# Fourier mixing and a hardswish MLP on one core: the first pair of batches reordered, weights converted in pairs and two phases, forward rows on SP's queue, scratch writes by Scalar

## The chip, the core and the metric

The kernel runs on one core of a Trainium2 chip. The metric is the device time of one execution in microseconds (us), the median of several runs, lower is better. TensorE does the matmuls (PE in the profile, PEld its weight loads), DVE is VectorE, ACT is ScalarE, POOL is GpSimd, SP the engine that mostly issues transfers. The granted clock is the share of TensorE's full clock that the profile records for a stretch; 0.50 is called half clock below. The DMA share is the mean busy share of the core's 16 DMA engines, so the share times 16 is a number of engines; it can come out slightly above 1.

## The reference

A two-dimensional Fourier transform over sequence and features, of which the real part goes through a two-layer MLP:

```python
X = np.fft.fft(x, axis=1)              # x: (8, 3008, 256) float32
X = np.fft.fft(X, axis=2)
h = X.real.reshape(24064, 256) @ w_in  # w_in: (256, 2048)
g = h * np.clip(h + 3.0, 0.0, 6.0) / 6.0
out = g @ w_out                        # w_out: (2048, 256)
```

The weights arrive as float64. The kernel computes in float32, so it takes their bits apart with integer operations and puts float32 together ("narrowing").

## The kernel before

The sequence length is split as 47 x 64. Batches are worked in four pairs. For a pair, **stage 1** transforms over 47 in eight pieces; each piece needs four forward rows of x and four mirrored ones for 94 row groups (2 batches x 47). The mirrored ones come by an indirect transfer, the "gather". The result z goes to a scratch in DRAM (`zd`), is read back transposed (`g`), and **stage 2** finishes the transform. The feature transform is folded into w_in beforehand. The MLP then runs in steps: `mlp1` (first layer and gating), `combine` on POOL, `mlp2` (second layer, by a seven-product scheme whose mixed weights are `G`). Later pairs' stage 1 runs beside the MLP of the pair before; only the first pair stands alone, and the conversion of all weights falls into that time.

```python
def load_x(pr, c):                       # two x buffers, both transfers on POOL's queue
    xt = xpool.tile([PR, 2 * XC, D], F32, tag="x", name="xt")      # PR = 94
    nc.gpsimd.dma_start(out=xt[:, 0:n, :], in_=rows[:, c * XC + 1:c * XC + 1 + n, :])
    ...
    nc.gpsimd.indirect_dma_start(out=xt[:, XC:, :]..., in_=x_r,
        in_offset=bass.IndirectOffsetOnAxis(ap=IX[:, i:i + 1], axis=0))

def narrow(st, o):                       # one tile of weights, eight operations, all on DVE
    ts(top[:], hi, 0xFFFFF, 0x100000, op0=AL.bitwise_and, op1=AL.bitwise_or)
    ts(low[:], lo, 8, 0xFFFFFF, op0=AL.logical_shift_right, op1=AL.bitwise_and)
    stt(frac[:], low[:], 2.0 ** -24, top[:], op0=AL.mult, op1=AL.add)
    ts(ex[:], hi, 20, 0x7FF, op0=AL.logical_shift_right, op1=AL.bitwise_and)
    ts(ex[:], ex[:], 1023.0 - 127.0, 0.0, op0=AL.subtract, op1=AL.max)
    ts(ex[:], ex[:], 255.0, 2.0 ** 23, op0=AL.min, op1=AL.mult)
    stt(ex[:], hi, -2 ** 31, ex[:], op0=AL.bitwise_and, op1=AL.bitwise_or)
    stt(o, frac[:], 2.0 ** -20, ex[:].bitcast(F32), op0=AL.mult, op1=AL.mult)

for c in range(NXC):                     # stage 1 of the first pair; NXC = 8
    for part, eng in enumerate((nc.gpsimd, nc.vector)):
        fold(first, c, part, eng)        # add forward and mirrored rows: POOL, then DVE (y)
    if c + 2 < NXC:
        load_x(first, c + 2)
    for i in range(XC // 2):
        stage1(first, c, i)              # TensorE, copy of z by ACT, scratch write by SP
    narrow_w_in(c)
    ...
```

After stage 1 come the first two w_out tiles, stage 2, and the main loop; the other six w_out tiles are narrowed one per step in steps 0 to 5. In the timelines shown here POOL, DVE and Scalar each work through their own instructions in program order.

Of the kernel before, what the change touches and what calls it, by code (L numbers as in the profile page):

```python
# [40 lines left out]

N1, N2 = 47, 64
# [6 lines left out]
def kernel(  # L49
# [10 lines left out]
    nc = tc.nc  # L60
# [19 lines left out]
    xpool = ctx.enter_context(tc.tile_pool(name="xpool", bufs=2))  # L80
# [21 lines left out]
    T = consts.tile([P, 2, NK1, 2, N2], F32, name="T")  # L102
# [14 lines left out]



    def load_x(pr, c):  # L120
        xt = xpool.tile([PR, 2 * XC, D], F32, tag="x", name="xt")
        rows = x_pn[pr.p * PR:(pr.p + 1) * PR]
        n = XC if c < NXC - 1 else XC - 1
        nc.gpsimd.dma_start(out=xt[:, 0:n, :], in_=rows[:, c * XC + 1:c * XC + 1 + n, :])
        if n < XC:
            nc.gpsimd.dma_start(out=xt[:, n:XC, :], in_=rows[:, 0:1, :])
        i = pr.p * NXC + c
        nc.gpsimd.indirect_dma_start(
            out=xt[:, XC:, :].rearrange("p n d -> p (n d)"), out_offset=None, in_=x_r,
            in_offset=bass.IndirectOffsetOnAxis(ap=IX[:, i:i + 1], axis=0),  # L130
        )
        pr.x[c] = xt

    def fold(pr, c, part, eng):
        xt = pr.x[c]
        n = XC if c < NXC - 1 else XC - 1
        a, r = xt[:, 0:n, :], xt[:, 2 * XC - 1:2 * XC - 1 - n:-1, :]
# [7 lines left out]
        lo, hi = xt[:, 0:XC, 1:P], xt[:, 0:XC, D - 1:P:-1]  # L145
# [3 lines left out]
        if n < XC:  # L149
            h = xt[:, XC, :]  # L150
            tt(y[:, XC, 1:P], h[:, 1:P], h[:, D - 1:P:-1], op=AL.add)
            tt(y[:, XC, P + 1:D], h[:, 1:P], h[:, D - 1:P:-1], op=AL.subtract)
            eng.tensor_copy(y[:, XC, 0:P + 1:P], h[:, 0:P + 1:P])
            eng.tensor_copy(y[:, n, 0:P + 1:P], xt[:, n, 0:P + 1:P])
# [10 lines left out]
    def stage1(pr, c, i):  # L165
# [18 lines left out]
        if i == XC // 2 - 1:  # L184
            nc.sync.dma_start(
                out=pr.zd[:].rearrange("b k c n d -> (b k c) n d")[:, c * XC:(c + 1) * XC, :],
                in_=z[:],
            )
            del pr.y[c], pr.z[c]
# [11 lines left out]
    def stage2(pr, gr, i):  # L201
# [5 lines left out]
        for u in range(2):  # L207
            kk = 2 * i + u
            for blk in range(2):
                nc.tensor.matmul(ps[:, blk, 2 * u:2 * u + 2], g[:, kk, blk * P:(blk + 1) * P],  # L210
                                 T[:, blk, gr * 2 * KK + kk], start=True, stop=True)
        nc.scalar.copy(pr.q[gr][:, :, 4 * i:4 * i + 4, :], ps[:])

    def stage2n_mul(pr, gr):

        shape = [P, 2 * KK, 2 * N2]
        m = spool.tile(shape, F32, tag="m", name="m")
        t0 = T[:, 0, gr * 2 * KK:(gr + 1) * 2 * KK].rearrange("p k b n -> p k (b n)")
        nc.gpsimd.tensor_tensor(m[:], t0, pr.g[gr][:, :, P:P + 1].to_broadcast(shape), op=AL.mult)
        pr.pr[gr] = m  # L220

    def stage2n_sum(pr, gr):
        m = pr.pr.pop(gr)
        ps = bank([P, 2 * TB], "ps3")
        nc.tensor.matmul(ps[:], ones[:], m[:].rearrange("p k n -> p (k n)"), start=True, stop=True)  # L225
# [74 lines left out]
    def mlp2(ch, fc):  # L300
# [3 lines left out]
        for i, mv in enumerate(moving):  # L304
# [5 lines left out]
            if fc == NF - 1 and (i % 2 == 1 or i == 6):  # L310
# [3 lines left out]
                nc.scalar.copy(ch.e[:, k:i + 1, 0:ch.n], ch.acc[i // 2][:, 0:i + 1 - k, 0:ch.n])  # L314
# [37 lines left out]
    nc.sync.dma_start(out=F[:], in_=c_stage1)  # L352
    nc.vector.tensor_copy(IX[:], F[0:PR, 5 * PZ:])
    for c in range(2):
        load_x(first, c)
    nc.sync.dma_start(out=C[:], in_=c_dim.rearrange("(h p) d -> p h d", p=P))
# [3 lines left out]
    wide = moe_w_in.dtype != F32  # L360
    WB = 512

    def load_w(src, dst):
        if not wide:
            nc.sync.dma_start(out=dst, in_=src)
            return None
        st = wpool.tile([P, 2 * WB], I32, tag="st", bufs=3, name="st")
        o = st[:].bitcast(moe_w_in.dtype)
        if len(src.shape) == 3:
            o = o.rearrange("p (c j) -> p c j", c=src.shape[1])  # L370
        nc.sync.dma_start(out=o, in_=src)
        return st

    def narrow(st, o):


        if st is None:
            return
        words = st[:].rearrange("p (n two) -> p n two", two=2)
        lo, hi = words[:, :, 0], words[:, :, 1]  # L380
        ts, stt = nc.vector.tensor_scalar, nc.vector.scalar_tensor_tensor
        top = wpool.tile([P, WB], I32, tag="top", name="top")
        low = wpool.tile([P, WB], I32, tag="low", name="low")
        ex = wpool.tile([P, WB], I32, tag="ex", name="ex")
        frac = wpool.tile([P, WB], F32, tag="frac", name="frac")
        ts(top[:], hi, 0xFFFFF, 0x100000, op0=AL.bitwise_and, op1=AL.bitwise_or)
        ts(low[:], lo, 8, 0xFFFFFF, op0=AL.logical_shift_right, op1=AL.bitwise_and)  # L387
        stt(frac[:], low[:], 2.0 ** -24, top[:], op0=AL.mult, op1=AL.add)  # L388
        ts(ex[:], hi, 20, 0x7FF, op0=AL.logical_shift_right, op1=AL.bitwise_and)
        ts(ex[:], ex[:], 1023.0 - 127.0, 0.0, op0=AL.subtract, op1=AL.max)  # L390
        ts(ex[:], ex[:], 255.0, 2.0 ** 23, op0=AL.min, op1=AL.mult)
        stt(ex[:], hi, -2 ** 31, ex[:], op0=AL.bitwise_and, op1=AL.bitwise_or)  # L392
        stt(o, frac[:], 2.0 ** -20, ex[:].bitcast(F32), op0=AL.mult, op1=AL.mult)

    w_in = {}

    def load_w_in(j):
        n, i = j // 2, j % 2
        w = wpool.tile([P, WB], F32, tag="w", bufs=5, name="w_in")
        w_in[n, i] = w, load_w(moe_w_in[i * P:(i + 1) * P, n * WB:(n + 1) * WB], w[:])  # L400

    def narrow_w_in(j):
        w, st = w_in[j // 2, j % 2]
        narrow(st, w[:])


    w_out = {}

    def load_w_out(j):
        w = wpool.tile([P, WB], F32, tag="w", bufs=5, name="w_out")  # L410
        rows = moe_w_out[2 * j * P:2 * (j + 1) * P, :].rearrange("(c p) d -> p c d", p=P)
        w_out[j] = w, load_w(rows, w[:].rearrange("p (c d) -> p c d", c=2))

    def narrow_w_out(j):
        w, st = w_out[j]
        narrow(st, w[:])

    def mix_w_out(j):
        bs = [w_out[j + i * (NWO // 2)][0][:].rearrange("p (c q h e) -> h p c q e", c=2, h=2, e=DH) for i in range(2)]
        b11, b12, b21, b22 = bs[0][0], bs[0][1], bs[1][0], bs[1][1]  # L420
        w = [G[:, i, 2 * j:2 * j + 2, :].rearrange("p c (q e) -> p c q e", e=DH) for i in range(7)]
        t2 = wpool.tile([P, 2, DB, DH], F32, tag="t2", name="t2")
        tt = nc.vector.tensor_tensor
        nc.scalar.copy(w[0], b11)
        nc.scalar.copy(w[1], b21)
        nc.scalar.copy(w[6], b22)
        tt(w[3], b11, b12, op=AL.subtract)
        tt(t2[:], b22, w[3], op=AL.add)
        tt(w[2], t2[:], b21, op=AL.subtract)
        tt(w[4], b22, b12, op=AL.subtract)  # L430
        nc.scalar.mul(w[5], t2[:], -1.0)

    NWI, NWO = 2 * FF // WB, NFC // 2
    for j in range(2):
        load_w_in(j)
    for b in range(2):
        nc.vector.memset(T[(1 - b) * N2:(2 - b) * N2, :, :, b], 0.0)
        nc.scalar.dma_start(out=T[b * N2:(b + 1) * N2, :, :, b], in_=c_stage2)
    nc.vector.memset(half[:], 0.5)
    nc.gpsimd.memset(ones[:], 1.0)  # L440

    def fold_w_in(n):

        cs = slice(n * 512, (n + 1) * 512)
        for blk in range(2):
            ps = bank([P, 512], "wps")
            for i in range(2):
                nc.tensor.matmul(ps[:], C[:, i, blk * P:(blk + 1) * P], w_in[n, i][0][:],
                                 start=(i == 0), stop=(i == 1))
            nc.scalar.copy(W1[:, blk, cs], ps[:])  # L450
        ps = bank([P, 512], "wns")
        for j in range(512 // P):
            for i in range(2):
                nc.tensor.matmul(ps[:, j:j + 1], w_in[n, i][0][:, j * P:(j + 1) * P], C[:, i, D:D + 1],
                                 start=(i == 0), stop=(i == 1))
        nc.scalar.copy(WN[:, n * (512 // P):(n + 1) * (512 // P)], ps[:, 0:512 // P])

    for c in range(NXC):
        for part, eng in enumerate((nc.gpsimd, nc.vector)):
            fold(first, c, part, eng)  # L460
        if c + 2 < NXC:
            load_x(first, c + 2)
        for i in range(XC // 2):
            stage1(first, c, i)
        narrow_w_in(c)
        if c + 2 < NWI:
            load_w_in(c + 2)
        if c % 2:
            fold_w_in(c // 2)
    ORDER = [0, NWO // 2, 1, NWO // 2 + 1, 2, NWO // 2 + 2, 3, NWO // 2 + 3]  # L470
    for j in ORDER[0:2]:
        load_w_out(j)
    load_g(first, 0)
    load_g(first, 1)
    for i in range(2):
# [3 lines left out]
    for j in range(2):  # L479
        narrow_w_out(ORDER[j])  # L480
        load_w_out(ORDER[j + 2])
    mix_w_out(0)
# [6 lines left out]
    def beside(p):  # L489
# [6 lines left out]
        if p == 0:  # L496
            for j in range(2, NWO):
                put(j - 2, narrow_w_out, ORDER[j])
                if j + 2 < NWO:
                    put(j - 2, load_w_out, ORDER[j + 2])  # L500
                if j % 2:
                    put(j - 2, mix_w_out, j // 2)
# [61 lines left out]
def _tables(B, S, D):  # L564
# [14 lines left out]
    for b in range(2):  # L579
# [21 lines left out]
        "c_stage2": t.reshape(N2, 2, NK1, N2).astype(np.float32),  # L601
        "c_dim": d.astype(np.float32),
# [32 lines left out]
```

## Time and profile before

| | before |
|---|---|
| time, median of 3 runs first given | 2096.5 us (2095.32 to 2096.98) |
| TensorE busy | 1985.9 us, 95% of the span |
| TensorE busy, first 200 us | 110.9 us |
| last fold result y of stage 1 | 98.4 us |
| first gating on DVE | 120.1 us |
| second layer of step 6 (seventh `acc` group) starts | 198.7 us |

From about 200 us on TensorE is full (199.32 us busy of the 200 from 400 to 600 us, at a granted clock of 1.00) and the rest of the work is fixed, so the three last rows serve as mile marks throughout. I call the stretch to the first mark part A, between the first and second part M, between the second and third part B. (The first mark is the start of the last but one DVE operation of the last y, always the same one; the prediction counts from an operation some 0.3 us earlier, 98.1.) Lines of this profile stand in the prediction.

### The profile page before, as it was taken

The page shows a single profiled execution, that of the slowest core. Times are in us where ns is not written, and L with a number is a line of the kernel's source. Part 1 is how long each engine was busy: PE and PEld are TensorE (multiplying, and loading weights), DVE is VectorE, ACT ScalarE, POOL GpSimd, SP SyncE. Part 2 cuts the span into 40 slices and gives each one's busy share as a digit, 9 for nine tenths or more (in the row PEclk, how much of TensorE's full clock was granted, in tenths as well). Part 3 has the DMA queues.
Part 4 walks back from the last instruction along what each step waited for, and adds up shares of the span by engine and source line. Part 5 has one row for each costly group of instructions (what it writes and reads, how often), then busy time and mean ns, then how long its engine had stood idle before and what let it go on. Part 6 is the DMA issues. An engine that isn't in the chain of part 4 may idle for free.

```text
span 2095.7 us, 28082 instructions
## 1 busy us (share of the span) xinstructions
PE 1985.9 (95%) x9136; PEld 1698.7 (81%) x9136; DVE 1495.8 (71%) x2768; ACT 671.6 (32%) x1157; POOL 1474.1 (70%) x1637
## 2 busy tenths in 40 slices
PE   3666999999999999999999999999999999999997
PEld 1355888888888888888888888888888888888886
DVE  4588676777677677667677667777677777777775
ACT  1122333333333333333333333333333333333332
POOL 3333887788667788778767787787866766766765
PEclk9678999999999999999999999999999999999999
DMA  6430121112101112112101111111020010010000
GB/s 160 133 110 10 43 54 48 50 37 49 28 21 34 43 33 61 47 38 52 35 21 30 42 38 43 42 51 47 23 48 11 14 26 21 16 26 21 16 16 19
DMA packets 163377, 86.81 MB, mean 41 GB/s; under 512 B 138496, under 2 KB 151040, under 8 KB 163232
## 3 DMA queue, kind: packets, MB, share of 16 engines
q1 hardware_dynamic: 128896, 58.71, 11.4%
q0 software_dynamic: 28160, 24.73, 4.4%
q10 hardware_dynamic: 6176, 1.57, 0.4%
q8 instruction: 74, 1.21, 0.3%
q14 instruction: 71, 0.58, 0.1%
HBM read 47.65 MB, written 37.22 MB: 40 GB/s over the span
## 4 chain that ended last, share of the span: by engine, by line
PE 88%; DVE 5%; DMA 4%; ACT 1%; POOL 1%; issue 1%; SPq 0%; DVEq 0%; POOLq 0%; ACTq 0%
PE acc L308 52%; PE v L254 15%; PE u L254 15%; DMA xt<-in_x_dram,IX 3%; PE ps L210 2%; PE ps L182 2%; DVE a L286 1%; PE ps L225 1%; ACT t L283 1%; DVE u L267 1%; DVE s L259 0%; DVE frac L388 0%; DVE low L387 0%; DMA g<-zd 0%; DVE ex L392 0%
## 5 line engine op out<-in xcount | busy, mean ns | idle before, releaser
L298 POOL TENSOR_TENSOR c<-a 128x512 f32<-128x512 f32 (+1 forms) x384 | 479.2, 1248 | 447.2 <-DVE a L286 257.2
L308 PE MATMUL acc<-c,G 128*128 128x256 f32 (+1 forms) x3072 | 714.0, 375 | 0.0
L308 PEld LDWEIGHTS acc<-c,G 128*128 128x128 f32 x3072 | 579.7, 191 | 73.9
L283 ACT ACTIVATE t<-u,half 128x512 f32<-128x512 f32 (+2 forms) x416 | 272.2, 654 | 1102.5 <-DVE u L267 1090.8
L259 DVE SCALAR_TENSOR_TENSOR s<-qn,WN,u 128x256 f32<-128x256 f32 x768 | 334.7, 477 | 365.1 <-PE u L254 364.5
L308 PE MATMUL acc<-a,G 128*128 128x256 f32 (+1 forms) x2304 | 557.5, 379 | 0.0
L308 PEld LDWEIGHTS acc<-a,G 128*128 128x128 f32 x2304 | 439.8, 192 | 58.7
L254 PE MATMUL v<-q,W 128*128 128x256 f32 x1536 | 402.3, 385 | 31.7 <-DVE a L286 31.7
L254 PE MATMUL u<-q,W 128*128 128x256 f32 x1536 | 395.0, 379 | 0.0
L254 PEld LDWEIGHTS v<-q,W 128*128 128x128 f32 x1536 | 292.6, 192 | 80.3 <-issue 35.3
L254 PEld LDWEIGHTS u<-q,W 128*128 128x128 f32 x1536 | 287.9, 190 | 65.8 <-issue 20.7
L286 DVE SCALAR_TENSOR_TENSOR a<-t,u 128x512 f32<-128x512 f32 (+2 forms) x416 | 266.2, 646 | 99.2 <-ACT t L283 94.0
L298 POOL TENSOR_TENSOR c<-a,c 128x256 f32<-128x256 f32 (+1 forms) x384 | 276.2, 719 | 30.1
L298 POOL TENSOR_TENSOR c<-c,a 128x256 f32<-128x256 f32 (+1 forms) x384 | 274.9, 716 | 30.1
L267 DVE TENSOR_TENSOR u<-s,v 128x512 f32<-128x512 f32 (+1 forms) x384 | 263.0, 685 | 41.1 <-PE v L254 1.3
L283 ACT ACTIVATE t<-v,half 128x512 f32<-128x512 f32 (+1 forms) x384 | 256.9, 669 | 5.5 <-DVE v L273 4.5
L273 DVE TENSOR_TENSOR v<-v,s 128x512 f32<-128x512 f32 (+1 forms) x384 | 257.7, 671 | 1.1
L286 DVE SCALAR_TENSOR_TENSOR a<-t,v 128x512 f32<-128x512 f32 (+1 forms) x416 | 255.1, 620 | 0.4 <-ACT t L283 0.2
L182 PE MATMUL ps<-y,F 94*96 94x512 f32 x120 | 73.7, 712 | 59.9 <-DVE y L148 53.8
L298 POOL TENSOR_TENSOR r<-w,e 128x256 f32<-128x256 f32 (+1 forms) x96 | 92.2, 981 | 3.8
L314 ACT COPY e<-acc 128x512 f32<-128x512 f32 (+1 forms) x192 | 86.3, 540 | 2.9 <-PE acc L308 2.8
L182 PEld LDWEIGHTS ps<-y,F 94*96 94x96 f32 x120 | 20.7, 186 | 80.3 <-issue 34.3
(68 smaller groups left out, 856.3 us busy)
## 6 DMA issues: line engine op xcount, KB each, us to landing
out_dram<-o SPq DMA_DIRECT2D x736, 32.0 KB, 1.6
zd<-z SPq DMA_DIRECT2D x32, 384.0 KB, 3.0
g<-zd SPq DMA_DIRECT2D x48, 256.0 KB, 3.9
xt<-in_x_dram POOLq DMA_DIRECT2D x28, 376.0 KB, 4.0
st<-in_moe_w_in_dram SPq DMA_DIRECT2D x8, 512.0 KB, 10.2
st<-in_moe_w_out_dram SPq DMA_DIRECT2D x8, 512.0 KB, 6.0
T<-in_c_stage_dram ACTq DMA_DIRECT2D x2, 768.0 KB, 25.5
xt<-in_x_dram POOLq DMA_DIRECT2D x4, 282.0 KB, 3.4
```

Source lines behind the costliest of these rows:

```text
L182: nc.tensor.matmul(ps[0:PZ], F[0:PR, 0:PZ], y[:, 2 * i:2 * i + 2, :], start=True, stop=True)
L210: nc.tensor.matmul(ps[:, blk, 2 * u:2 * u + 2], g[:, kk, blk * P:(blk + 1) * P], T[:, blk, gr * 2 * KK + kk], start=True, stop=True)
L225: nc.tensor.matmul(ps[:], ones[:], m[:].rearrange("p k n -> p (k n)"), start=True, stop=True)
L254: nc.tensor.matmul(ps[:, i], W1[:, blk, f * P:(f + 1) * P], q[:, blk, of:of + KC], start=True, stop=True)
L259: nc.vector.scalar_tensor_tensor(s[:, i].rearrange("p k n -> p (k n)"), qn[:, of * N2:(of + KC) * N2], WN[:, f:f + 1], u[:, i].rearrange(" ...
L267: nc.vector.tensor_tensor(u[:, :, 0:ns], s[:, :, 0:ns], v[:, :, 0:ns], op=AL.add)
L273: nc.vector.tensor_tensor(v[:, :, 0:nm], v[:, :, 0:nm], s[:, :, 0:nm], op=AL.subtract)
L283: nc.scalar.activation(t, h, AF.Relu, bias=half[:], scale=scale)
L286: nc.vector.scalar_tensor_tensor(dst, t, 1.0, h, op0=AL.min, op1=AL.mult)
L298: nc.gpsimd.tensor_tensor(out, in0, in1, op=AL.add)
L308: nc.tensor.matmul(ch.acc[i // 2][:, i % 2, 0:ch.n], G[:, i, fc, :], mv, start=(fc == 0 and i % 2 == 0), stop=(fc == NF - 1), skip_group_c ...
L314: nc.scalar.copy(ch.e[:, k:i + 1, 0:ch.n], ch.acc[i // 2][:, 0:i + 1 - k, 0:ch.n])
```

## The change

The intent: fetch x three pieces ahead and not two; take rows and scratch writes off the queues on which they made others wait; take work off DVE by giving the exponent to Scalar (phase one) and the final multiply to POOL (after phase two), two tiles at a time so that one tile's DVE work covers the other's Scalar work; and convert weights only shortly before they are needed.

```diff
-    xpool = ctx.enter_context(tc.tile_pool(name="xpool", bufs=2))
+    xpool = ctx.enter_context(tc.tile_pool(name="xpool", bufs=4))   # half-size tiles, and 9 borrowed
 def load_x(pr, c):
+        nr, eng = (PR + 2, nc.sync) if pr.p == 0 else (PR, nc.gpsimd)
-        nc.gpsimd.dma_start(out=xt[:, 0:n, :], ...)
+        eng.dma_start(out=xt[0:nr, 0:n, :], ...)
         nc.gpsimd.indirect_dma_start(...)                       # gather: still 94 rows
 def stage1(pr, c, i):
         nc.scalar.copy(z[:, 2 * i:2 * i + 2, :], ps[0:PZ])
-            nc.sync.dma_start(
+            (nc.scalar if pr.p == 0 else nc.sync).dma_start(    # scratch write
+    def narrow_a(j):
+        ts(ex[:], hi, 20, 0x7FF, op0=AL.logical_shift_right, op1=AL.bitwise_and)
+        nc.scalar.activation(exf, ex[:], AF.Relu, bias=bias[:, 0:1], scale=1.0)
+        nc.scalar.activation(exf, exf, AF.Relu, bias=bias[:, 1:2], scale=-1.0)
+        nc.scalar.activation(ex[:], exf, AF.Identity, bias=bias[:, 2:3], scale=-2.0 ** 23)
+        ts(top[:], ...); ts(low[:], ...); nc.vector.scalar_tensor_tensor(frac, ...)
+    def narrow_b(j):
+        nc.vector.scalar_tensor_tensor(ex[:], hi, -2 ** 31, ex[:], op0=AL.bitwise_and, op1=AL.bitwise_or)
+        nc.gpsimd.tensor_tensor(o, frac, ex[:].bitcast(F32), op=AL.mult)
+    def mix_w_out(j):                                           # subtractions now on POOL
+        nc.scalar.copy(g[0], b11); nc.scalar.copy(g[1], b21); nc.scalar.copy(g[6], b22)
+        tt(g[3], ...); tt(g[5], ...); tt(g[2], ...); tt(g[4], ...)
+        nc.scalar.mul(g[5], g[5], -1.0)
+    narrow_pair(0); use_pair(0)                                 # ahead of the first fold
     for c in range(NXC):
         fold(first, c, 0, nc.gpsimd); fold(first, c, 1, nc.vector)
+        if c + 3 < NXC: load_x(first, c + 3)
+        if c < 6: load_w(c + 2)
         for i in range(XC // 2): stage1(first, c, i)
-        narrow_w_in(c) ...
+        if c in (2, 5):
+            narrow_pair((c + 1) // 3); use_pair((c + 1) // 3)
+    ... narrow_pair(3); stage 2; use_pair(3)
+    # main loop: pairs 4 to 7 in steps 0, 1, 3 and 5
```

(`narrow_pair(j)` runs `narrow_a` and then `narrow_b` for the two tiles of pair j; `use_pair(j)` folds a pair of w_in into the feature transform or mixes a pair of w_out. Cut: the constants T are loaded in six parts instead of two at the start, and the factor 2^-20 of the conversion moves into the tables and the last copy.)

## The prediction

The 4.8 us of DVE a pair come from, for each of two tiles, three operations at 0.34 us and two at 0.69 us.

> **What bounds the kernel now.** I read the page's slices first, then the busy table by stretch, then the chain of work in order of time for the first 215 us, then the timeline of that stretch. In the slices (columns: 40 equal parts of the span, about 52 us each):
>
> ```profile
> PE   3666999999999999999999999999999999999997
> ...
> DVE  4588676777677677667677667777677777777775
> ...
> PEclk9678999999999999999999999999999999999999
> ```
>
> TensorE is full from the fifth slice to the last but one. So the change, which touches only the first pair of batches, can gain only in the first four slices, some 200 us; after them the kernel needs the same matmuls as now. The busy table by stretch shows the two regimes (columns: stretch; its length; busy us and counts of PE, PEld, DVE, ACT, POOL; granted clock; DMA share; GB/s):
>
> ```profile
> 140.00:160.00 20.00, 13.50 (x50) 10.76 (x48) 18.93 (x29) 2.50 (x5) 8.02 (x8) 0.79 0.13 40
> ...
> 400.00:600.00 200.00, 199.32 (x931) 172.51 (x931) 142.70 (x256) 67.25 (x113) 152.06 (x171) 1.00 0.15 38
> ```
>
> The start has two parts with different limits. **Part A**, 0 to 98 us, is stage 1 over eight pieces of x. The chain (start, duration, what) is made of the mirrored-row gathers:
>
> ```profile
> 4.09 19.33 DMA xt<-in_x_dram,IX
> ...
> 28.70 15.88 DMA xt<-in_x_dram,IX
> ...
> 57.64 16.05 DMA xt<-in_x_dram,IX
> ...
> 80.04 14.81 DMA xt<-in_x_dram,IX
> ...
> 103.46 3.12 DMA zd<-z
> ...
> 107.44 6.61 DMA g<-zd
> ```
>
> Two buffers let piece c+2 be fetched only when piece c is folded, so each round of latency plus work passes two pieces. The first fold result y is done at 27.2 and the last at 98.1: 10.1 us a piece. **Part M**, 98 to 120 us, is the last stage-1 piece, the scratch write and read, stage 2, and the first mixed w_out weights on DVE. **Part B**, 120 to 199 us, is the first steps of the main loop. Each step waits for one weight conversion on DVE, all eight operations in a row:
>
> ```profile
> 174.06 0.34 DVE top L386
> 174.40 1.42 DVE low L387
> 175.84 1.10 DVE frac L388
> 176.94 0.88 DVE ex L389
> 177.84 1.38 DVE ex L390
> 179.24 1.38 DVE ex L391
> 180.64 0.70 DVE ex L392
> 181.37 0.69 DVE w_out L393
> ```
>
> That is 8.0 us here; the same eight take about 4.0 us where nothing disturbs them. With 3.7 us of gating work per step, DVE needs 11 to 12 us a step where TensorE needs 4.75 us (14 matmuls in 3.02 us plus eight in 1.73 us).
>
> [...] (columns as above):
>
> ```profile
> 20.00:24.00 4.00, 0.00 (x0) 0.00 (x0) 0.00 (x0) 0.00 (x0) 0.43 (x1) 1.00 0.26 100
> 90.00:95.00 5.00, 3.70 (x4) 0.96 (x4) 4.23 (x10) 1.16 (x2) 0.08 (x1) 0.54 0.11 45
> ```
>
> While two gathers are in flight and nothing else, the share is 0.26, or 4.2 of 16 engines, at 100 GB/s; with one it is 0.11, about two engines, at 45 GB/s. So a gather of 376 KB needs at least some 7.5 us, but several gathers run side by side on different engines. [...] gathers take 15 to 16 us while SP's queue is busy, and 11.5 us at 218 us, where it is quieter. [...] L387 takes 0.35 us at 48.7 us and 1.42 us in the list above, with POOL combining at that time. [...] The granted clock here is 0.50 in 50 to 60 us and 1.00 once TensorE is full[...].
>
> **Part A after the change.** Removed: 1.5 MB of T, which competed from 0.74 us; the two-buffer limit (13 x tiles before the first reuse, three pieces ahead); the forward rows from POOL's queue; three of eight DVE operations per conversion. Added: two conversions before the first fold, and 1.25 us of POOL multiply per converted tile (the duration of L298's 128x512 row), two tiles a pair. DVE per pair: [...] 4.8 us a pair. The exponent takes three ACT operations of 0.65 us, hidden by the other tile.
>
> POOL's order makes the clock. Gathers 0, 1 and 2 go out at 4, 6 and 8 us and land at about 20, 22 and 24 (16 us, as now under load). The first pair of w lands at about 10 (now 9.2 us after issue), converted by 15 to 17, so it does not hold up fold 0. Fold is 2.3 us on POOL, a gather about 1.9 us to issue: fold 0 at 20 to 22.3, fold 1 to 26.5, fold 2 to 30.7. POOL then waits for DVE's second pair (y done at 32.1, plus 5.5, multiplies until 39.2); gather 3, sent at 22.6, has landed at 38.6. Fold 3 to 41.5, fold 4 to 45.7, fold 5 to 49.9. Third pair and its mixing: DVE until 56, two multiplies, four additions of 0.72 on POOL, until 61. Fold 6 to 63.3, fold 7 to 65.1, the last y at **66.6** against 98.1. Gain 31.5 us. The bytes allow it: about 14 MB until then, at the 250 GB/s of the full stretches, are 56 us, which leaves little room.
>
> **Part M.** Now 20.4 us pass from the last y (98.1) to the first main matmul (118.56). After: reads of scratch no longer stand beside 1 MB of w_out, so about 2 us less; but the fold of the fourth pair (8 wide and 16 narrow matmuls, plus copies, about 5.2 us) now stands between stage 2 and the first main matmul. So 23.7 us: first main matmul at 90.3, first DVE gating at **92** against 120.2. Gain 28 us.
>
> **Part B.** Counted from that first gating, now mlp2 of step 6 starts at +78.5 (198.7 less 120.2). After, by steps: two gatings, 7.4. Pair 4 on DVE until 12.9; POOL multiplies until 14.2; its fold on TensorE through one PSUM bank (three evacuations between) until 21.5; gating of step 2 until 26. Pair 5 until 31, multiplies and mixing on POOL until 36, combine of step 2 until 39.5. Pair 6 with some blocking by POOL until 46, mixing until 50.4, combine of step 4 until 53. Pair 7 until 60, mixing until 65, combine of step 6 until 67.8. So mlp2 of step 6 at **+68**, gain 10.5 us. Four pairs at about 5 us are 20 us of DVE in place of six tiles at about 7.5, 45 us; over half of that goes into the new POOL and PSUM links of this chain.
>
> **Sum.** 31.5 less 3.3 plus 10.5 is 38.7; 2096.5 less 38.7 is 2057.8, rounded to **2057**.
>
> **Rivals.** (1) Bandwidth binds part A. For it: the byte count above, and every gather leans on two engines that also serve SP's long backlog. If gathers take 20 us instead of 16, part A ends at about 75 and the time is about 2066. Against it: the DMA share is mostly 0.5 in 20 to 100 us. (2) Part B gains more: if POOL's mixing and the single PSUM bank cost less than I chained, DVE alone would need 8 gatings at 3.7 and 20 us, +50 instead of +68; time about 2040. Against: combine is behind mixing in POOL's order. (3) POOL becomes the bound in part B, with multiplies and mixing delaying combine[...]: +76 and about 2066. (4) The start was hidden anyway and nothing moves, 2096: the chain speaks against it, as it leads through these gathers and conversions, and nothing later is waiting.
>
> **Range and chances.** Each of parts A and B may miss by some 8 to 10 us either way, M by 3; together about 13 us, so 2040 to 2074. Faster by over 2% means below 2054.6, just under my middle: 0.42. Slower by over 2% would need a new stall of 80 us: 0.01. The rest, 0.57, within 2%.
>
> **What would show it.** Right: the last DVE y at about 67 us, gathers about 15 us but three in flight; the first gating at about 92; mlp2 of step 6 at about 160, with POOL's multiply and mixing before combine on the chain, a gap on TensorE around the fold of pair 4; DVE conversions of about 5 us a pair; everything after it shifted by one constant. Wrong: gathers above 20 us on the chain, or waits for w, a gating that starts on time but proceeds at 11 us a step, or a steady stage whose step is not 4.75 us.

Measured figures to set beside the prediction, from the kernel before unless another is named:

- Two gathers side by side had a DMA share of 0.26, one alone 0.13 (450 to 452 us). The 7.5 us for a gather is an estimate, 376 KB at half of the 100 GB/s; the shortest of the 32 gathers took 11.3 us.
- That the gathers' engines also serve SP's list is seen in the changed kernel: SP's queue took 100.5% of the 16 engines' time from 3 to 9 us, while the first three gathers were issued.
- The 250 GB/s are an estimate: 266 GB/s from 4 to 12 us, 168 from 12 to 20 (shares of 1.12 and 1.02).
- Eight undisturbed conversion operations took 4.2 us (from 109.35 us). Scalar's 128x512 operations took 0.69 us, those of the exponent 0.72 in the changed kernel.
- A read of `g` took 7.0 us beside the w_out loads and 3.9 from 300 to 1000 us. Eight wide and 16 narrow matmuls took 7.0 us from 39.06 us.
- Four matmuls that take 1.03 us on a full TensorE took 2.04 or 2.05 us after five of the six waits of 3.8 to 4.9 us between 133 and 199 us, and 1.50 us after the other.

## The result, and the profile after

The changed kernel took 2092.52 us (median of 4 runs, 2091.89 to 2092.86) against 2096.53 us before (median of 4). The ratio is 0.9981, 95% interval 0.9964 to 0.9999. The gain is real and small, 4 us, where 39 were predicted; the time lies outside the range.

The slices of the changed kernel, the same three rows as in the prediction:

```profile
PE   3467999999999999999999999999999999999997
...
DVE  4446766777677677767677677677677777777775
...
PEclk7578999999999999999999999999999999999999
```

and its busy table for the two stretches shown there (stretch, length, busy us and counts of PE, PEld, DVE, ACT, POOL, clock, DMA share, GB/s):

```profile
140.00:160.00 20.00, 15.45 (x63) 12.89 (x64) 13.11 (x25) 8.42 (x15) 8.71 (x10) 0.81 0.41 115
...
400.00:600.00 200.00, 199.32 (x931) 172.53 (x930) 142.34 (x256) 67.15 (x112) 151.82 (x170) 1.00 0.17 39
```

The steady state is the same to the last digit of TensorE's time. In the start DVE has been relieved as intended, 13.1 us of 20 instead of 18.9. But TensorE is hardly fuller, and no engine is full in that stretch: time goes in waits from engine to engine. The gathers that made the chain of before have their answer in POOL's timeline of the changed kernel (start, duration, line, operation, and in brackets how long POOL had stood idle and for what):

```profile
7.81 4.17 POOL L141 DMA_INDIRECT xt<-in_x_dram,IX  x1 [0.30 <-issue]
...
30.55 1.25 POOL L153 TENSOR_TENSOR xt<-xt 94x508 f32<-94x508 f32 x1 [12.83 <-DMA xt<-in_x_dram,IX]
...
54.12 1.27 POOL L410 TENSOR_TENSOR st<-top,ex 128x512 f32<-128x512 f32 x1 [9.34 <-DVE ex L408]
...
80.00 1.26 POOL L410 TENSOR_TENSOR st<-top,ex 128x512 f32<-128x512 f32 x1 [11.39 <-DVE ex L408]
```

POOL begins to send the third of the first gathers at 7.8 us and is done with it at 12.0, yet the first fold starts at 30.5 (23.6 in the kernel before). Later, POOL stands twice for some 10 us at the multiply (L410) of a weight pair, with the next folds behind it in its order. What the multiply waits for is seen in Scalar's timeline:

```profile
48.35 0.58 ACT L196 COPY z<-ps 96x512 f32<-96x512 f32 x1 [1.13 <-PE ps L195]
50.06 0.58 ACT L196 COPY z<-ps 96x512 f32<-96x512 f32 x1 [1.13 <-PE ps L195]
50.67 0.31 ACTq L198 DMA_DIRECT2D zd<-z  x1
51.08 0.72 ACT L398 ACTIVATE ex<-ex,bias 128x512 f32<-128x512 int32 x1 [0.44 <-ACT z L196]
```

DVE had the exponent bits ready at 45.0. Scalar turns to them at 51.1, as the copies of z for pieces 1 and 2 stand ahead in its order and wait for TensorE, which runs at half clock there (0.50 from 44 to 52 us). So a ring forms: fold (POOL), y (DVE), stage 1 (TensorE), copy (ACT), exponent (ACT), second phase (DVE), multiply (POOL), next fold.

In part B, DVE's timeline of the changed kernel answers to the conversion of the kernel before:

```profile
149.53 0.69 DVE L408 SCALAR_TENSOR_TENSOR ex<-st,ex 128x512 int32<-128x512 int32 x1
150.90 1.22 DVE L408 SCALAR_TENSOR_TENSOR ex<-st,ex 128x512 int32<-128x512 int32 x1 [0.68 <-ACT ex L400]
...
156.88 0.69 DVE L300 SCALAR_TENSOR_TENSOR a<-t,u 128x512 f32<-128x512 f32 x1 [2.57 <-ACT t L297]
```

This pair of tiles began at 146.06 and was done at 152.1: 6.1 us for two where one took 8.0. But then the gating stands 2.57 us for its relu, the part of it that Scalar does. Scalar had this in front of it, the mixing of weights:

```profile
155.85 0.42 ACT L438 ACTIVATE G<-G 128x256 f32<-128x256 f32 x1 [1.59 <-POOL G L436]
156.17 0.67 ACT L297 ACTIVATE t<-u,half 128x512 f32<-128x512 f32 x1
```

| mile mark (us) | before | predicted | after |
|---|---|---|---|
| last y | 98.4 | 66.6 | 93.1 |
| first gating | 120.1 | 92 | 119.0 |
| second layer of step 6 | 198.7 | 160 | 194.4 |

### The profile page after: what moved, and what is told of

The parts are those of the page before. It is cut to its first block, busy times and chain, and to the rows that moved or that the text cites. A ratio compares the mean times of both kernels' runs of the same rounds, so it can differ in the third digit from the quotient of the medians.

```text
span 2090.5 us, 28142 instructions
## 1 busy us (share of the span) xinstructions
PE 1978.4 (95%) x9136; PEld 1692.8 (81%) x9136; DVE 1455.1 (70%) x2707; ACT 706.7 (34%) x1205; POOL 1499.2 (72%) x1660
## 4 chain that ended last, share of the span: by engine, by line
PE 89%; DVE 3%; ACT 1%; issue 1%; POOL 1%; DMA 0%; SPq 0%; DVEq 0%; POOLq 0%; ACTq 0%
PE acc L322 53%; PE v L268 16%; PE u L268 15%; PE ps L195 2%; PE ps L223 2%; PE ps L239 1%; DVE a L300 1%; ACT t L297 1%; PE wps L447 0%; DVE u L281 0%; DVE s L273 0%; DVE o L348 0%; POOL st L410 0%; DVE v L287 0%; PE ps L192 0%
## 5 line engine op out<-in xcount | busy, mean ns | idle before, releaser
L328 ACT ACTIVATE e<-acc 128x512 f32<-128x512 f32 (+1 forms) x192 | 86.9, 543 | 2.9 <-PE acc L322 2.8
L348 DVE STREAM_TRANSPOSE o<-r 128x256 f32<-128x256 f32 (+1 forms) x192 | 72.5, 416 | 6.5 <-POOL r L312 6.4
```

The lines of the kernel that those rows point to most:

```text
L328: nc.scalar.mul(ch.e[:, k:i + 1, 0:ch.n], ch.acc[i // 2][:, 0:i + 1 - k, 0:ch.n], 1.0 / WS)
L348: nc.vector.transpose(o[:, 0:n // DH, h], ch.r[:, m, h, 0:n].rearrange("p (j i) -> p j i", i=DH))
```

## The experiments

Ten kernels, each timed in 3 rounds beside the kernel before. All gave correct results. E1, E2, E4 and E5 ran on one chip, E3, E6, E7 and E8 on a second, E9 and E10 on a third; the kernel before took 2096.9 us on each, so medians can be compared to 2 or 3 us. "Changed" is the kernel after the change. Marks are from the profiled runs.

| kernel | last y | first gating | step 6 | part B | time, us | ratio to before (95%) |
|---|---|---|---|---|---|---|
| before | 98.4 | 120.1 | 198.7 | 78.6 | 2096.9 | |
| changed | 93.1 | 119.0 | 194.4 | 75.4 | 2092.5 | 0.9981 (0.9964 to 0.9999) |
| E1 Scalar's order in stage 1 | 86.7 | 114.0 | 191.9 | 77.9 | 2088.4 | 0.9958 (0.9942 to 0.9975) |
| E2 scratch writes on SP again | 89.2 | 118.4 | 193.7 | 75.2 | 2092.2 | 0.9977 (0.9960 to 0.9993) |
| E3 forward rows on POOL again | 83.4 | 109.6 | 184.8 | 75.2 | 2082.5 | 0.9931 (0.9915 to 0.9948) |
| E4 gather of 96 rows | 77.1 | 103.3 | 178.5 | 75.2 | 2077.3 | 0.9909 (0.9892 to 0.9926) |
| E5 mixing behind the relus | 93.5 | 119.7 | 191.0 | 71.3 | 2090.1 | 0.9978 (0.9961 to 0.9994) |
| E6 before, gather of 96 rows | 74.9 | 96.0 | 173.4 | 77.4 | 2070.5 | 0.9871 (0.9854 to 0.9887) |
| E7 phases one piece apart | 81.7 | 106.4 | 181.7 | 75.2 | 2079.6 | 0.9916 (0.9899 to 0.9932) |
| E8 = E4 + E7 + E5 | 65.3 | 90.1 | 161.1 | 71.0 | 2060.2 | 0.9830 (0.9814 to 0.9847) |
| E9 = E8, pair 4 before the loop | 63.8 | 97.8 | 153.5 | 55.7 | 2055.0 | 0.9801 (0.9785 to 0.9818) |
| E10 = E8, rows on POOL | 66.4 | 90.7 | 161.7 | 71.0 | 2064.3 | 0.9848 (0.9831 to 0.9864) |

**E1, Scalar's order.** The theory was that Scalar's order is the link that makes POOL stand still.

```diff
+        if c in (2, 5):
+            narrow_pair((c + 1) // 3)
         for i in range(XC // 2):
             stage1(first, c, i)
         if c in (2, 5):
-            narrow_pair((c + 1) // 3)
             use_pair((c + 1) // 3)
```

> Against the changed kernel, only Scalar's order differs: in stage 1 the exponent operations of the second and third pair of weights stand before the copies of z of pieces 2 and 5, not behind them. Theory (Scalar's queue is the link: the conversion waits behind copies that wait for stage 1 on TensorE at half clock, and POOL's next fold waits behind the conversion's multiply): POOL's two waits of 9.3 and 11.4 us for DVE L408 fall to about 4 us each, the last y comes some 10 us earlier (about 82 us), the time is about 2082. Rival (the gathers and DMA set the pace of part A anyway): POOL waits for gathers instead, the last y stays above 88 us and the time within 3 us of 2092.5.

The waits fell from 9.34 to 5.92 us and from 11.39 to 7.98, the last y came 6.4 us earlier, the time fell by 4.1. The direction is the theory's, the size two fifths of it. Scalar's timeline says why: the exponent now starts at 48.1 instead of 51.1, behind the copies of piece 1 instead of piece 2; those still wait for TensorE. Moving it one piece up is not taking it out of the ring. Part B also became 2.5 us longer in this run. One group of four matmuls there took 3.78 us at a clock of 0.51, where it had taken 1.98 at 1.00; what the rest is was not settled.

**E2, scratch writes back on SP.** This undoes one part of the change and at the same time holds SP back.

```diff
-            (nc.scalar if pr.p == 0 else nc.sync).dma_start(
+            nc.sync.dma_start(
```

> One part of the change undone: the scratch writes of the first pair go back to SP's queue, so that SP stops at the first of them until z of piece 0 is there and cannot send the later rows and weights ahead. Theory (the first gathers take 26 to 30 us because SP sends its whole list in the first 11 us): the first gather lands by about 22 us instead of 30.5 and the time gains up to 6 us, if the later rows do not come too late; rows or weights that come late on SP would eat this. Rival (the gathers are slow for a reason of their own, two engines whatever else runs): first gather still at about 30 us, time 2092 or longer.

The first fold started at 23.9 us instead of 30.5. So SP's early list does slow the first gathers; in the changed kernel the DMA share from 4 to 24 us is 1.05, in E2 0.75. The time did not move, for the reason that the expectation had named: weights came late. DVE's timeline in E2, at the second tile of the second pair:

```profile
48.47 0.43 DVE L397 TENSOR_SCALAR ex<-st 128x512 int32<-128x512 int32 x1 [9.73 <-DMA st<-in_moe_w_in_dram]
```

POOL's wait for that pair grew to 13.9 us, and part M to 29.2 us. One link was shortened and the next took it up.

**E3, forward rows back on POOL's queue.**

```diff
-        nr, eng = (PR + 2, nc.sync) if pr.p == 0 else (PR, nc.gpsimd)
+        nr, eng = PR, nc.gpsimd
```

> One part of the change undone: the forward rows of the first pair go back to POOL's queue, 94 rows each. Theory (SP's rows and weights sent in the first 11 us are what the first gathers compete with): with 3 MB less ahead on SP, paced by POOL's order now, the first gather lands a little earlier than 30.5 us (about 24), but POOL spends 0.9 us more per piece, so the time stays within 5 us of 2092. Rival (HWDGE rows are what made the change gain anything): gathers wait behind the rows in POOL's queue, land after 30 us, and the time goes back to 2097 or more.

Neither expectation held: the time fell by 10 us, to 2082.5. The first gather landed earlier as expected, POOL's timeline of E3 having

```profile
22.37 1.26 POOL L153 TENSOR_TENSOR xt<-xt 94x508 f32<-94x508 f32 x1 [4.86 <-DMA xt<-in_x_dram,IX]
```

and POOL's next wait shrank as well (9.34 to 6.65 us). This time nothing gave it back, since the weights, now alone on SP, came in time (up to 115 us no engine is listed as waiting for them). So this part of the change, as it stood, cost 10 us.

**E4, a gather of 96 rows.** Two unused rows are added. That a gather of 96 rows would run on more engines than one of 94 was the estimate here; the shares under E6 are the first to show it.

```diff
-    IX = consts.tile([PR, NP * NXC], I32, name="IX")
+    IX = consts.tile([PR + 2, NP * NXC], I32, name="IX")
-    nc.vector.tensor_copy(IX[:], F[0:PR, 5 * PZ:])
+    nc.vector.tensor_copy(IX[:], F[:, 5 * PZ:])
-            out=xr[0:PR].rearrange("p n d -> p (n d)"), ...
+            out=xr[:].rearrange("p n d -> p (n d)"), ...
```

> The gather asks for 96 rows instead of 94 (the two added rows are read and never used), nothing else differs from the changed kernel. Theory (94 rows go to two DMA engines[...]): the gathers land within 10 us of their issue even under the backlog, the first fold starts at about 18 us instead of 30.5, later gathers take under 8 us, and the time falls by about 10 us to 2082. Rival (the backlog of all 16 engines is what delays them[...]): first gather still lands after 25 us, and time within 3 us of 2092.5.

Measured: 2077.3, 15 us less than the changed kernel. The median time to landing of the first three gathers, in the changed kernel and then in E4 (queue, operation, count, us):

```profile
xt<-in_x_dram,IX POOLq DMA_INDIRECT x3, 28.4
```

```profile
xt<-in_x_dram,IX POOLq DMA_INDIRECT x3, 11.6
```

That is more than the expected 10 us to landing, but soon enough: the first fold starts at 17.5 us, right behind the first pair's multiplies, 13.1 us earlier. POOL also needs less time to issue a later gather, 1.3 to 1.4 us instead of 1.9. POOL waits for no gather in the first 115 us; it waits 10.3 and 11.4 us for L408, as in the changed kernel. The last y moved by 16.0 us, the time by 15.2: a shift that passes to the end nearly whole.

**E5, mixing behind the relus.**

```diff
     def mix_w_out(j):
-        nc.scalar.copy(g[0], b11); nc.scalar.copy(g[1], b21); nc.scalar.copy(g[6], b22)
         tt(g[3], ...); tt(g[5], ...); tt(g[2], ...); tt(g[4], ...)
-        nc.scalar.mul(g[5], g[5], -1.0)
+        late.append(scalar_part)        # these four, run after the step's mlp1
```

> In the main loop Scalar's part of the mixing of w_out (three copies and the negation, which waits for POOL's additions) is issued behind the two relus of the step instead of ahead of them; everything else as in the changed kernel. Theory (Scalar's order holds up the relu, and with it DVE and TensorE, at each of three mixings): the three waits of DVE a for ACT t of 2.6, 3.0 and 2.1 us vanish, the seventh step's second matmul group starts about 7 us earlier after the first gating (at +68 instead of +75.4), and the time is about 2085. Rival (the mixing itself on POOL, ahead of combine, sets the pace): combine still comes late, TensorE then waits for combine or G, and the gain is under 3 us.

Who waited for whom from 140 to 200 us (total us, times, longest), changed kernel and then E5:

```profile
DVE a L300 <- ACT t L297: 8.5, 7, 3.0
```

```profile
DVE a L300 <- ACT t L297: 1.2, 7, 0.2
```

The waits went as the theory said. Part B shortened by 4 us, not 7, and the median time by 2.4. That is the size that the rival had named, but not its mechanism: TensorE does not wait for `combine` or `G`; it still waits 3.5 to 4.8 us for the gating three times, now at the conversion itself. The gain in time is not clear of noise: three runs took 2089.4 to 2090.5 us and one 2096.5, and the ratio, 0.9978, is that of the changed kernel within its interval. The 4 us of part B are read from one profiled run.

**E6, the kernel before with a gather of 96 rows.** The same edit as E4 on the kernel before (its x tile grows by two rows for it), with nothing of the change.

> The kernel before, with nothing of the change, but its gather asks for 96 rows instead of 94. Theory (part A of the kernel before is four rounds of a 15 to 16 us gather that runs on two DMA engines): each round falls by 6 to 9 us, the last y comes at about 70 us instead of 98, and the time is about 2068, more than the whole change brought. Rival (the 94 rows matter only under the changed kernel's backlog on SP): under 8 us of gain, 2089 or more.

Measured 2070.5, 26 us less than before and 22 less than the changed kernel, close to the theory's 2068. Between 300 and 1000 us, where the engines are quiet, gathers land in this time, kernel before and then E6:

```profile
xt<-in_x_dram,IX POOLq DMA_INDIRECT x13, 12.0
```

```profile
xt<-in_x_dram,IX POOLq DMA_INDIRECT x12, 4.8
```

Two rows more, 2% more bytes, and well under half the time. The forward rows on the same queue stay at 3.7 to 3.9 us in both. The number of engines can be read where a gather runs alone, in the kernel before and then in E6 (columns as in the busy table):

```profile
450.00:452.00 2.00, 2.00 (x15) 1.87 (x14) 1.17 (x2) 0.37 (x1) 0.69 (x1) 1.00 0.13 53
```

```profile
422.00:423.00 1.00, 1.00 (x6) 0.87 (x6) 0.90 (x3) 0.00 (x0) 0.84 (x2) 1.00 0.59 217
```

A share of 0.13 is two engines of 16; in E6 it is over nine even in the tail of a gather. POOL's own time to issue a gather in stage 1 fell too, from 1.5 to 1.7 us to 0.95 to 1.15, so a small part of the gain may be that.

**E7, the two phases one piece apart.** Phase one at pieces 2 and 5 ahead of Scalar's copies, phase two and the multiply at pieces 3 and 6 behind the folds.

```diff
+        for i in range(2):
+            if c in (3, 6):
+                narrow_b(2 * (c // 3) + i)
+        for i in range(2):
+            if c in (2, 5):
+                narrow_a(2 * ((c + 1) // 3) + i)
         for i in range(XC // 2):
             stage1(first, c, i)
-        if c in (2, 5):
-            narrow_pair((c + 1) // 3); use_pair((c + 1) // 3)
+        if c in (3, 6):
+            use_pair(c // 3)
```

> The changed kernel with the two phases of the second and third pair of weights put one piece apart in stage 1: the first phase ahead of the copies of piece 2 (5), the second phase with POOL's multiply behind the folds of piece 3 (6). Theory (POOL stands still for 9.3 and 11.4 us because its multiply, which waits for DVE and Scalar, stands ahead of the next fold): both waits for L408 fall under 1 us; fold 3 then waits for its gather until about 48 us, so the first gives back about 9 us and the second about 10; the last y at about 75 us, the time about 2078. Rival (with those waits gone the gathers on two engines hold the pace): waits for gathers of 10 us and more, last y at 85 or later, time 2087 or more.

Measured 2079.6, 13 us less; the theory had 2078. The last y came at 81.7 us, between the theory's 75 and the rival's 85. POOL's timeline in E7:

```profile
49.25 1.25 POOL L153 TENSOR_TENSOR xt<-xt 94x508 f32<-94x508 f32 x1 [4.03 <-DMA xt<-in_x_dram,IX]
...
53.68 2.82 POOL L410 TENSOR_TENSOR st<-top,ex 128x512 f32<-128x512 f32 x2
```

The multiply of the second pair no longer waits (9.34 before), and the fold in front of it now waits 4.03 us for its gather. So the rival has a share: part of the gain goes over to the gathers.

**E8, the three together** (E4, E7 and E5).

> The changed kernel with 96 rows in the gather, the two phases one piece apart in stage 1, and Scalar's part of the mixing behind the relus. If the three causes are separate links of one chain, the gains add up: about 15 for the gather, some 15 to 18 more for POOL's two waits, which nothing hides any more, and 2 to 3 for the mixing: about 2058, last y near 57 us. If they hide each other, or stage 1 on TensorE at half clock takes over (eight pieces at about 3.6 us and two folds of weights at 7 us are 43 us): 2066 or more.

Measured 2060.2. The single gains were 15.2, 12.9 and 2.4 us, in sum 30.5; together they are 32.3. So they behave as separate links, within the spread of E8's runs (three within 2059.0 to 2060.2, one 2065.3). The marks are now where the prediction had put them, 65.3, 90.1 and 161.1 against 66.6, 92 and 160; here the first gating and the second layer of step 6 in DVE's and TensorE's timelines:

```profile
90.09 0.87 DVE L273 SCALAR_TENSOR_TENSOR s<-qn,WN,u 128x256 f32<-128x256 f32 x2 [14.31 <-PE u L268]
```

```profile
161.08 1.98 PE L322 MATMUL acc<-a,G 128*128 128x256 f32 x6
```

The last y, however, had been expected near 57 in this run. POOL's timeline of E8 shows that the multiply of the third pair still waits:

```profile
55.43 1.26 POOL L411 TENSOR_TENSOR st<-top,ex 128x512 f32<-128x512 f32 x1 [7.98 <-DVE ex L409]
```

The second pair's waits 2.57 us. Over the longer wait TensorE runs twelve matmuls of stage 1 without a gap, from 47.6 to 58.2 us, at a granted clock of 0.50. So the rival, stage 1 at half clock, has a share as well, and no run here takes it away.

**E9, the fourth later pair before the main loop.** The last of w_in is converted while TensorE waits for the scratch.

```diff
     narrow_pair(3)
+    narrow_pair(4)
     ... stage 2 ...
     use_pair(3)
+    use_pair(4)
     # main loop: the pair of step 0 is left out
```

> The kernel of the last combination (96-row gather, phases apart, mixing late: 2060) with the fourth later pair, the last of w_in, converted and folded just before the main loop, while TensorE waits for the scratch to come back, instead of in its first step. Theory (in part B the fold of that pair waits for DVE, Scalar and POOL in turn and then evacuates one PSUM bank three times, 19 us from the second gating to the next first matmul): the first gating comes about 5 us later (95 instead of 90) but the seventh second-layer group falls from +71 to about +55 after it, and the time to about 2050. Rival (that stretch was covered by the two steps worked ahead, or the later pairs wait longer instead): under 3 us of gain, 2057 or more.

First gating 7.7 us later, part B 55.7 instead of 71.0 us, and the time 2055.0 (2052.5 to 2056.3): 5 us less, somewhat short of the 2050 expected. It is the fastest version tried, faster than both kernels, with a ratio at the edge of 2%.

**E10, rows back on POOL in E8.**

> The same combination (2060) with the forward rows of the first pair on POOL's queue again, 94 rows a transfer. Under the changed kernel this undoing gave 10 us, because the first gather landed at 22 instead of 30.5. If the rows on SP hurt only through the two-engine gather, then with 96 rows in the gather it should now cost POOL 0.9 us a piece and bring nothing: 2060 to 2068. If the rows on SP hurt by themselves (they fill all engines ahead of everything), the time should again fall by some 5 to 10 us, to 2053.

Measured 2064.3. Its runs fall in two groups (2061 and 2062, 2067 and 2067), E8's also reach from 2059.0 to 2065.3 on another chip, so a difference of 4 us is not resolved. What can be said: the undoing no longer gains 10 us. With the 96-row gather the rows on SP do no harm that these runs show, and no clear good.

## Why the prediction was wrong

**What held.** TensorE is full behind the start, nothing there changed, and what is won before the third mark is won almost in full. Part M was right: 25.4 us from the last y to the first gating predicted, 25.9 measured. Pair 4 in part B was right: the next first matmul at +21.5 predicted, and it came 22.0 us after the first gating (141.0 less 119.0). The slow cases of its rivals (1) and (3) had the right places: rival (1), gathers of 20 us under SP's backlog, was too mild, as the first three took 28.4; rival (3) had +76 for part B, and 75.4 was measured, though Scalar had a share in it that the rival did not name. Gathers above 20 us were also named as a sign of being wrong, and were seen.

**The steps that failed** are two in part A and one in part B. Part A ended 26.5 us later than predicted, part B took 7.4 us more, part M 0.5 more: 34.4 of the 35.5 us by which the time was missed.

First, "Gathers 0, 1 and 2 ... land at about 20, 22 and 24 (16 us, as now under load)". They took 26.4 us and more, median 28.4. The same prediction had counted that a gather runs on two engines (a share of 0.13 where one runs alone) and that these serve SP's backlog too (SP's queue took 100.5% of the 16 engines' time from 3 to 9 us in the changed kernel), and then took the latency of the kernel before, in which SP sends four transfers by 2.7 us and is then held back until 31.7. Under the change SP sends 14 in its first 11 us; the term was taken from the wrong load. The chain shown with the prediction even has 19.33 us for the first gather, the one beside the loads of the start. The first fold began at 30.5 instead of 20: 10.5 us. Three runs agree: less on SP (E2: 23.9; E3: 22.4), two more rows in the gather (E4: 17.5).

Second, "POOL then waits for DVE's second pair (y done at 32.1, plus 5.5 ...)". This took the pair as DVE work with Scalar's part "hidden by the other tile". In the first pair, where Scalar was free, that nearly held: DVE waited 0.53 us for it. For the later pairs Scalar's own order was not looked at: the copies of z stood in it, and these waited for stage 1, which ran at half clock. Scalar turned to the exponent 6.1 us after DVE had it ready in the second pair, and 6.6 us in the third (70.4 to 77.0). POOL's waits were 9.3 and 11.4 us where the working implies 4.1 and about 5.6, so 11 us lost, and E7 gave back 11.5 us at the first mark by taking the multiply out of that place. E1 shows that Scalar's order is the link, but only in part.

What the half clock itself costs, no run separates. With these two the first mark is explained to about 5 us (26.5 less 21.5). POOL's timeline shows the rest in small pieces against the working: a wait of 1.1 us for the second gather, gaps of 0.8 and 0.9 us between the two multiplies of a pair, 0.2 us more at each of the other folds but one, and about 1.2 us more in fold 7 and from it to the last y.

Third, in part B, "combine of step 6 until 67.8" had POOL's mixing on the path but not Scalar's share of it, which stood ahead of the relus. E5 puts it at 4 of the 7.4 us. What the other 3 us are was not settled; matmul groups at half clock are seen (14 matmuls in 4.2 us instead of 3.02 at 143 us, at a granted clock of 0.50 until 145 us; four in 2.04 or 2.05 us instead of 1.03 after each of the three waits of 4.3 to 5.4 us from 152 to 193 us, at 0.50), but no run separates them.

**Where the expected gain went.** The three-pieces-ahead loads and the relief of DVE both happened (DVE busy 52.7 us instead of 74.6 between 120 and 200 us). The time went into two new waits of POOL, waits of the gating for Scalar, and first gathers that are slow beside SP's list. E8 eases these, leaves the change otherwise as it is, and lands at 2060, 3 us from the prediction. The agreement is good but partly luck: in E8 the first fold starts at 17.2 us, not at the predicted 20, and POOL's two waits are 2.6 and 8.0 us where the working implies 4.1 and about 5.6.

Two readings in the prediction are looser than it says. The stretch from 90 to 95 us, shown for one gather, also holds a scratch write (3.0 of its 11 points of share), and that from 20 to 24 the end of T's load (3.2 of 26). The conclusion of two engines for a gather stands by the stretch shown under E6 (0.13). And its sum, 2057.8, was rounded down.

One more reading was missed rather than wrong. The kernel before was bound in part A by a gather on two engines. The prediction read that from the trace (shares of 0.26 and 0.11) and then weighed the change's remedy, fetching further ahead. E6 shows what curing it directly was worth: two more rows bring 26 us, over six times the gain of the change.

## What to carry to other kernels

When work moves to another engine, write down that engine's whole order around the new place: here a short operation stood behind copies that waited for matmuls, and so became part of a ring. A latency from the profile belongs to the load it was measured under: here a gather took 12.0 us in the quiet stretch, 15 to 16 us beside SP's queue before and 28.4 us (the first three) beside SP's longer list. If the change removes what held a queue back, ask what its transfers will then compete with: here they filled the engines (100.5% from 3 to 9 us). And before hiding a slow transfer, look at how many DMA engines it uses: the DMA share times 16 while it runs alone says so (0.13, two engines, here), and a few more rows may be worth a trial, as going from 94 to 96 was here (12.0 to 4.8 us).

## What the traces show and leave open

- In the kernel before, a gather of 94 rows took 12.0 us from 300 to 1000 us, at a share of two engines (0.13); one of 96 rows took 4.8 us (E6), at over nine engines (0.59). Direct copies of 94 rows on the same queue took 3.9 and 3.7 us in the two kernels. Why the indirect transfer of 94 rows is the slow one was not shown.
- Three 94-row gathers beside SP's backlog took 28.4 us (median), more than twice the quiet 12.0. How the engines divide their time between the queues was not shown.
- In the changed kernel a DVE operation on 94x8 elements (L161), usually 0.17 us, took 3.21 us at 39.55 us and again at 65.45 us, and ended both times within 0.1 us of the end of the second of POOL's two folding operations (42.72 and 68.62 us). So it spans more than one POOL instruction. No run here tests the cause.
- In stage 1 of the changed kernel TensorE ran 94-row matmuls without a gap for 7.1 us from 42.9 us, and for 10.5 us from 47.6 us in E8, and the granted clock stayed at 0.50. Where 128-row matmuls ran without a gap from 55.5 us in the changed kernel, it was 0.50 until 59.4 us and 0.83 from 59.4 to 62.0 us. Why is open.
